# Scores of an attention in pieces of 512 and 256 keys instead of 384 and 384, contiguous in PSUM, with another order of the tasks

## The chip, the cores and the metric

One core of one Trainium2 chip. The metric is the device time of one execution in microseconds (us), lower is better. The times of the kernel before are the median of three runs; the trace is of one more execution, taken by the hardware profiler. TensorE is called PE in the rows, its weight loads PEld, VectorE DVE, ScalarE ACT, GpSimd POOL and SyncE, which issues the transfers, SP.

## The reference

```
kv_pool = kv.reshape(1, 96, 4, 8, 4, 128).mean(axis=(2, 4))   # 768 rows of 128
k = v = kv_pool.reshape(1, 768, 128) @ w_sr
s = (q @ k.T) / sqrt(128)                                     # q: 12288 x 128
a = exp(s - s.max(-1));  a /= a.sum(-1) + 1e-9
x = a @ v                                                     # 12288 x 128
h = x @ moe_w_in                                              # 128 -> 2048
g = where(h >= 1, h, where(h <= -1, 0, (h + 1)**2 / 4))
x2 = g @ moe_w_out                                            # 2048 -> 128
h2 = x2 @ moe2_w_in
out = (h2 * sigmoid(1.702 * h2)) @ moe2_w_out
```

All inputs and outputs are fp32.

## The kernel before

The 12288 queries are worked off in 24 **blocks** b of 512 (`TB`), each in four **tiles** t of 128 (`P`). All 768 keys (`NKEY`) stay on the chip as kT0 and kT1, a high and a low part. Nearly every product is split in this way for exactness: `mm3` (L349 to L352) does one product as three matmuls in fp32r, low times high, high times low, high times high (lines L350, L351, L352). Each matmul has its own load of a 128 x 128 stationary matrix.

For a tile of a block from the fourth on, `scores` (L729) does on TensorE `S_mm`: three matmuls on the first 384 keys (`HALF`) and three on the other 384, with the queries stationary. The tile S is one of three slots of two PSUM banks of 512 floats ("h" slots); each half stands at the beginning of a bank, so the tile is a [128, 2, 384] piece of a [128, 2, 512] slot. VectorE takes the row maximum (`S_max`, L743), ScalarE the exponential with its row sum (`S_exp`, L757). In `regular` ScalarE then writes the normalised high part Ph (L1125), VectorE the low part Pl (L1131), and VectorE transposes both in 32 x 32 squares into TT (L1140). SyncE sends each pair of tiles out to the array "turned" in device memory (L1161) and brings it back as PT_hi and PT_lo (L1173). TensorE then multiplies PT with V: that is pv of the block, which becomes x, split into xhi and xlo (L799, L346).

The MLPs follow with the same splits: h1 = x W1 into an h slot, 512 tokens x 256 hidden units at a time ("h1_8_7" is unit pair 7 of block 8), the activation u and its high and low parts ghi and glo on VectorE, ScalarE and GpSimd, and the product with O into an accumulator (acc1, L1244, L1245, L1247). The second MLP (h2, acc2) is alike. Blocks 0 to 3 take other paths: block 0 has code of its own with 384 keys at a time (S0_0x and S0_1x, maximum in L905, exponential in L912), blocks 1 to 3 write the exponentials over S in PSUM, transpose on TensorE and multiply in fp32 (L848). The weights (names W and O with the MLP's and the piece's number) are split on the chip while the first blocks run: conversions of a 128 x 512 piece in several steps on VectorE (L587, L593, L599, L606), ScalarE and GpSimd. Before all that, 4 x 4 patches of kv are summed (y, L414) and pooled on TensorE (L429, L431), and multiplied with w_sr (k_ps, L493, L521) to give kT (L502).

What order all this has on each engine is set by a planner before the program is built: each piece of work is a task with a key, and `Plan.order` takes for each engine the ready task with the least key for which its buffers are free by assumed durations:

```python
t.n, t.key = i, t.key + FINE.get(i, 0.0)
...
if best is None or (t.key, t.n) < (best.key, best.n):
    best = t
```

The keys come from a table `ORDER` (for instance `ATT_KEY` for the steps of the attention, `PAIR1` and `PAIR2` for those of the MLPs) and from `FINE`, one number for each of some thousand tasks.

Of the kernel before, what the change touches and what calls it, by code (L numbers as in the profile page):

```python
# [23 lines left out]
    REG_AT=2.93,  # L24
    STEP_AT=(0.54, 2.45, 0.5),
    ATT_KEY=(26.49, 2.85, 18.08, 13.03, -19.64, 10.84, 4.1, -15.3, 8.86, 57.26, -2.82),
    PAIR1=(3.65, -0.48, 3.27, 7.62, -6.74),
    PAIR2=(1.57, -6.31, 2.52, 13.5),
    ENDS=(7.48, -5.42),
# [1417 lines left out]
```

## Time and profile before

| | us |
|---|---|
| median of three runs (1303.97 to 1305.10) | 1304.73 |
| profiled execution, its own time | 1305.31 |
| its span from first to last instruction | 1303.6 |
| TensorE busy | 1291.9 (99%) |
| ScalarE busy | 1079.1 (83%) |
| GpSimd busy | 939.9 (72%) |
| VectorE busy | 910.2 (70%) |

The busy times are those of the whole span. A matmul's end is modelled in the trace and overlaps the next one's start, so what a matmul costs in a row of matmuls is read from one start to another. 5907 matmul records are in the trace; an fp32 matmul (L848, L429, L431, L864) leaves two.

### The profile page before, as it was taken

The page shows a single profiled execution, that of the slowest core. Times are in us where ns is not written, and L with a number is a line of the kernel's source. Part 1 is how long each engine was busy: PE and PEld are TensorE (multiplying, and loading weights), DVE is VectorE, ACT ScalarE, POOL GpSimd, SP SyncE. Part 2 cuts the span into 40 slices and gives each one's busy share as a digit, 9 for nine tenths or more (in the row PEclk, how much of TensorE's full clock was granted, in tenths as well). Part 3 has the DMA queues.
Part 4 walks back from the last instruction along what each step waited for, and adds up shares of the span by engine and source line. Part 5 has one row for each costly group of instructions (what it writes and reads, how often), then busy time and mean ns, then how long its engine had stood idle before and what let it go on. Part 6 is the DMA issues. An engine that isn't in the chain of part 4 may idle for free.

```text
span 1303.6 us, 16928 instructions
## 1 busy us (share of the span) xinstructions
PE 1291.9 (99%) x5907; PEld 1079.3 (83%) x5908; DVE 910.2 (70%) x1078; ACT 1079.1 (83%) x1265; POOL 939.9 (72%) x431
## 2 busy tenths in 40 slices
PE   9999999999999999999999999999999999999998
PEld 7868888888888888888888888888888888888886
DVE  4987676866777768767777677677776776775531
ACT  2878988888988888889888888898888888987765
POOL 4678886777766777777667767776677677766886
PEclk8999999999999999999999999999999999999999
DMA  9403155355445534554455344544553455333000
GB/s 339 147 9 93 22 172 135 105 150 148 124 114 168 133 111 114 150 146 117 113 170 136 108 120 146 144 115 113 170 138 105 128 146 144 100 106 105 1 9 17
DMA packets 166164, 157.42 MB, mean 121 GB/s; under 512 B 106304, under 2 KB 153024, under 8 KB 166080
## 3 DMA queue, kind: packets, MB, share of 16 engines
q1 hardware_dynamic: 165024, 156.21, 42.5%
q8 instruction: 48, 0.79, 0.3%
q14 instruction: 36, 0.29, 0.1%
q10 hardware_dynamic: 1056, 0.13, 0.1%
HBM read 85.52 MB, written 70.78 MB: 120 GB/s over the span
## 4 chain that ended last, share of the span: by engine, by line
PE 97%; DVE 1%; DMA 1%; issue 0%; SPq 0%; ACT 0%; DVEq 0%
PE h L350 13%; PE h L352 13%; PE h L351 13%; PE acc L1245 13%; PE acc L1247 13%; PE acc L1244 13%; PE S L350 3%; PE S L352 3%; PE S L351 3%; PE pv L352 2%; PE pv L351 2%; PE pv L350 2%; PE acc L1238 1%; PE pv L848 1%; DMA kv<-in_kv 1%
## 5 line engine op out<-in xcount | busy, mean ns | idle before, releaser
L346 POOL TENSOR_TENSOR glo<-u,ghi 128x1024 fp32r<-128x1024 f32 x350 | 837.0, 2409 | 300.4 <-ACT u L1334 135.1
L1274 DVE TENSOR_SCALAR u<-h 128x1024 f32<-128x1024 f32 x172 | 210.7, 1225 | 210.2 <-PE h L352 199.4
L1244 PE MATMUL acc<-ghi,O 128*128 128x512 f32 x752 | 293.7, 391 | 0.0
L1245 PE MATMUL acc<-ghi,O 128*128 128x512 f32 x752 | 293.3, 390 | 0.0
L1285 DVE SCALAR_TENSOR_TENSOR u<-h,u 128x1024 f32<-128x1024 f32 x192 | 233.7, 1218 | 82.1 <-ACT u L1281 76.1
L1328 ACT ACTIVATE ghi<-h 128x1024 fp32r<-128x1024 f32 x192 | 197.1, 1027 | 70.7 <-PE h L352 69.5
L1247 PE MATMUL acc<-glo,O 128*128 128x512 f32 x752 | 232.5, 390 | 0.0
L1281 ACT ACTIVATE u<-u 128x1024 f32<-128x1024 f32 x178 | 188.1, 1057 | 37.3 <-DVE u L1274 36.9
L1291 ACT ACTIVATE ghi<-u 128x1024 fp32r<-128x1024 f32 x184 | 194.8, 1060 | 7.2 <-PE acc L1245 3.5
L1334 ACT ACTIVATE u<-h 128x1024 f32<-128x1024 f32 x166 | 169.0, 1020 | 0.0
L1247 PEld LDWEIGHTS acc<-glo,O 128*128 128x128 f32 x752 | 141.1, 188 | 30.1
L1245 PEld LDWEIGHTS acc<-ghi,O 128*128 128x128 f32 x752 | 141.2, 188 | 27.3
L1244 PEld LDWEIGHTS acc<-ghi,O 128*128 128x128 f32 x752 | 141.2, 188 | 26.6
L350 PE MATMUL h<-xhi,W 128*128 128x512 f32 x384 | 151.2, 394 | 0.0
L351 PE MATMUL h<-xlo,W 128*128 128x512 f32 x384 | 149.7, 390 | 0.0
L352 PE MATMUL h<-xhi,W 128*128 128x512 f32 x384 | 149.7, 390 | 0.0
L351 PE MATMUL h<-x2lo,W 128*128 128x512 f32 x384 | 149.4, 389 | 0.0
L352 PE MATMUL h<-x2hi,W 128*128 128x512 f32 x384 | 149.4, 389 | 0.0
L350 PE MATMUL h<-x2hi,W 128*128 128x512 f32 x384 | 149.4, 389 | 0.0
L743 DVE TENSOR_REDUCE nm<-S 128x1 f32<-128x768 f32 x92 | 87.7, 953 | 9.3 <-PE S L352 7.0
L350 PEld LDWEIGHTS h<-xhi,W 128*128 128x128 f32 x384 | 72.1, 188 | 16.5 <-issue 1.3
L351 PEld LDWEIGHTS h<-xlo,W 128*128 128x128 f32 x384 | 72.1, 188 | 15.9 <-issue 0.7
(135 smaller groups left out, 1876.5 us busy)
## 6 DMA issues: line engine op xcount, KB each, us to landing
turned<-TT SPq DMA_DIRECT2D x82, 768.0 KB, 4.2
PT_lo<-turned SPq DMA_DIRECT2D x168, 192.0 KB, 4.6
PT_hi<-turned SPq DMA_DIRECT2D x160, 192.0 KB, 3.9
kv<-in_kv SPq DMA_DIRECT2D x12, 512.0 KB, 7.9
out<-o SPq DMA_DIRECT2D x94, 64.0 KB, 1.9
q<-in_q SPq DMA_DIRECT2D x92, 64.0 KB, 2.4
raw_W<-in_moe_w_in SPq DMA_DIRECT2D x8, 512.0 KB, 8.5
raw_O<-in_moe_w_out SPq DMA_DIRECT2D x8, 512.0 KB, 7.1
```

Of the source, the lines that this page charges most:

```text
L346: eng.tensor_tensor(out=lo, in0=full, in1=f32(hi), op=ALU.subtract)
L350: nc.tensor.matmul(ps, wl, xh, start=first, stop=False)
L351: nc.tensor.matmul(ps, wh, xl, start=False, stop=False)
L352: nc.tensor.matmul(ps, wh, xh, start=False, stop=last)
L1244: nc.tensor.matmul(acc, w[c][1], hi[:, c], start=k == 0 and c == 0, stop=False)
L1245: nc.tensor.matmul(acc, w[c][0], hi[:, c], start=False, stop=False)
L1247: nc.tensor.matmul(acc, w[c][0], lo[:, c], start=False, stop=k == NP - 1 and c == 1)
L1274: nc.vector.tensor_scalar(u, T["h", 1, b, k], -1.0, 1.0, ALU.max, ALU.add)
L1281: nc.scalar.activation(u, u, AF.Square, scale=1.0 if light else 0.5)
L1285: nc.vector.scalar_tensor_tensor(out=u, in0=T["h", 1, b, k], scalar=1.0, in1=u, op0=ALU.max, op1=ALU.min)
L1291: nc.scalar.activation(t, T["u", 1, b, k], AF.Copy)
L1328: nc.scalar.activation(t, T["h", 2, b, k], AF.Gelu_apprx_sigmoid)
```

## The change

The scores of a tile become three matmuls on keys 0 to 511 and three on keys 512 to 767. They now lie contiguous in the two banks, so that maximum, exponential, high and low part read one row of 768 in place of two of 384. Where the exponentials are written over S, the row sum goes into the last column of the second bank in place of the first. Block 0 keeps its halves of 384.

```diff
+    def flat(b, t):
+        return T["S", b, t].rearrange("p h k -> p (h k)")[:, :NKEY]
...
             for half in halves:
-                mm3(S[:, half, :HALF], cols, [k[:, half * HALF : (half + 1) * HALF] for k in kT], True, True)
+                r = slice(half * TB, min(NKEY, (half + 1) * TB))
+                mm3(flat(b, t)[:, r], cols, [k[:, r] for k in kT], True, True)
...
-            nc.vector.tensor_reduce(nm, T["S", b, t][:, :, :HALF], AX.XY, ALU.max, negate=True)
+            nc.vector.tensor_reduce(nm, flat(b, t), AX.X, ALU.max, negate=True)
...
-                sm = E[:, 0, 511:512]
-                p = E[:, :, :HALF]
+                sm = E[:, 1, TB - 1 : TB]
+                p = flat(b, t)
...
-            nc.scalar.activation(p, E[:, :, :HALF], AF.Exp, bias=T["nm", b, t], accum_out=sm)
+            nc.scalar.activation(p, flat(b, t), AF.Exp, bias=T["nm", b, t], accum_out=sm)
...
-                    nc.scalar.activation(
-                        p.rearrange("p (h k) -> p h k", h=2), T["S", b, t][:, :, :HALF], AF.Copy, scale=T["rd", b, t]
-                    )
+                    nc.scalar.activation(p, flat(b, t), AF.Copy, scale=T["rd", b, t])
...
-                        out=p.rearrange("p (h k) -> p h k", h=2), in0=T["S", b, t][:, :, :HALF],
-                        scalar=T["rd", b, t], in1=f32(T["Ph", b, t]).rearrange("p (h k) -> p h k", h=2),
+                        out=p, in0=flat(b, t), scalar=T["rd", b, t], in1=f32(T["Ph", b, t]),
```

Of the tables, `REG_AT`, `STEP_AT`, `ATT_KEY`, `PAIR1`, `PAIR2`, `ENDS` and the whole of `FINE` have new numbers; the assumed durations are the same:

```diff
-    ATT_KEY=(26.49, 2.85, 18.08, 13.03, -19.64, 10.84, 4.1, -15.3, 8.86, 57.26, -2.82),
-    PAIR1=(3.65, -0.48, 3.27, 7.62, -6.74),
+    ATT_KEY=(25.32, 1.79, -127.3, 116.38, -197.55, 82.12, -0.25, -285.85, -41.23, 2.7, -91.74),
+    PAIR1=(-299.59, 32.45, -80.73, -171.76, -17.68),
```

Some lines move by one to four: L350 to L352 of before are L351 to L353 of the change. What the numbers do is seen in the programs' instructions. In the order of before TensorE does 94 runs of score matmuls, 92 of one tile and 2 of two tiles in a row (four of them block 0's half tiles); in that of the change 83 runs, 70 of one and 13 of two.

First place: TensorE in block 10, tiles 2 and 3 (S10_2, S10_3). Before:

```order
L350 MATMUL S10_2_4472<-kT0_70,qlo10_4130 128x384
L351 MATMUL S10_2_4472<-kT1_71,qhi10_4126 128x384
L352 MATMUL S10_2_4472<-kT0_70,qhi10_4126 128x384
...
L1244 MATMUL acc1_8_4243<-ghi_4315,O11_609 128x512
...
L352 MATMUL h1_8_7_4494<-xhi8_3901,W13_577 128x512
L350 MATMUL S10_3_4505<-kT0_70,qlo10_4130 128x384
...
L352 MATMUL S10_3_4505<-kT0_70,qhi10_4126 128x384
L1244 MATMUL acc2_7_4445<-ghi_4443,O20_762 128x512
```

And in the change:

```order
L353 MATMUL S10_2_4481<-kT0_70,qhi10_4061 128x512
L351 MATMUL S10_2_4481<-kT0_70,qlo10_4080 128x256
L352 MATMUL S10_2_4481<-kT1_71,qhi10_4061 128x256
L353 MATMUL S10_2_4481<-kT0_70,qhi10_4061 128x256
L351 MATMUL S10_3_4490<-kT0_70,qlo10_4080 128x512
...
L353 MATMUL S10_3_4490<-kT0_70,qhi10_4061 128x256
L1244 MATMUL acc2_7_4445<-ghi_4443,O20_920 128x512
```

The twelve matmuls (six of acc1, six of h1) between the two tiles are gone from there. Blocks 6 to 10, 12, 14, 16, 18, 20, 21 and 23 are like this; elsewhere the tiles still stand apart.

Second place: TensorE, the first matmuls of pv10, the product of block 10's turned parts with V. Before they stand behind both first tiles of block 11:

```order
L352 MATMUL S11_1_4741<-kT0_70,qhi11_4601 128x384
...
L1245 MATMUL acc2_7_4445<-ghi_4713,O23_1180 128x512
L1247 MATMUL acc2_7_4445<-glo_4738,O23_1180 128x512 x2
L350 MATMUL pv10_4783<-PT10_hi_4407,V1_73 128x512
L351 MATMUL pv10_4783<-PT10_lo_4408,V0_72 128x512
```

In the change they stand between them, six matmuls of acc2 behind the first:

```order
L353 MATMUL S11_0_4706<-kT0_70,qhi11_4536 128x256
L1244 MATMUL acc2_7_4445<-ghi_4677,O22_1065 128x512
...
L1247 MATMUL acc2_7_4445<-glo_4696,O22_1065 128x512 x2
L351 MATMUL pv10_4728<-PT10_hi_4407,V1_73 128x512
L352 MATMUL pv10_4728<-PT10_lo_4408,V0_72 128x512
...
L351 MATMUL S11_1_4793<-kT0_70,qlo11_4551 128x512
```

From the beginning of S10_2 to pv10 there were 156 matmuls, 24 of them scores; now there are 120, 18 of them scores. Blocks 10, 12, 14, 16, 18 and 21 are like this.

Third place: TensorE at the start, block 0's scores of the first 384 keys, first half tiles (S0_00), and the pooling (pool_ps) of the last patches. Before:

```order
L429 MATMUL pool_ps_202<-pm_66,kv10_172 128x32 x4
L429 MATMUL pool_ps_202<-pm_66,kv11_181 128x32 x4
L431 MATMUL pool_ps_202<-pm_66,y9_212 128x32 x2
L431 MATMUL pool_ps_202<-pm_66,y10_221 128x32
L431 MATMUL pool_ps_202<-pm_66,y11_236 128x32
L350 MATMUL S0_00_255<-kT0_70,qlo0_240 128x384
```

In the change:

```order
L430 MATMUL pool_ps_202<-pm_66,kv10_172 128x32 x4
L351 MATMUL S0_00_234<-kT0_70,qlo0_231 128x384
...
L353 MATMUL S0_00_234<-kT0_70,qhi0_200 128x384
L432 MATMUL pool_ps_202<-pm_66,y9_212 128x32 x2
L432 MATMUL pool_ps_202<-pm_66,y10_221 128x32
L430 MATMUL pool_ps_202<-pm_66,kv11_181 128x32 x4
L494 MATMUL k_ps_266<-pT_260,wsr_68 128x256
L432 MATMUL pool_ps_202<-pm_66,y11_241 128x32
```

The six score matmuls go ahead of the last patches. On VectorE, the last conversions and maxima ahead of xlo0 (the low part of block 0's x), before:

```order
L606 SCALAR_TENSOR_TENSOR f_556<-raw_W13_407,i_494 128x512
...
L599 SCALAR_TENSOR_TENSOR i_563<-raw_O11_364,i_563 128x512
L606 SCALAR_TENSOR_TENSOR O1f_336<-raw_O11_364,i_563 128x512
L743 TENSOR_REDUCE nm_599<-S2_1_579 128x1
L346 TENSOR_TENSOR xlo0_591<-A0_1_444,xhi0_590 128x512
```

In the change:

```order
L600 SCALAR_TENSOR_TENSOR i_509<-raw_O21_348,i_509 128x512
...
L607 SCALAR_TENSOR_TENSOR f_575<-raw_O21_348,i_509 128x512
L347 TENSOR_TENSOR xlo0_562<-A0_1_446,xhi0_561 128x512
L747 TENSOR_REDUCE nm_588<-S2_0_564 128x1
```

The maximum of block 2's score tile stands behind xlo0 now; between the last part of kT and xlo0 VectorE had 20 conversion steps of 128 x 512, now 17. On TensorE, the ten matmuls that begin block 1's pv (L864, L848) stood just ahead of block 0's first h1 and stand behind it now.

## Rows read from the trace of the kernel before

**Rows 1.** The page: busy time by engine; the chain that ended last.

```profile
PE 1291.9 (99%) x5907; PEld 1079.3 (83%) x5908; DVE 910.2 (70%) x1078; ACT 1079.1 (83%) x1265; POOL 939.9 (72%) x431
...
PE 97%; DVE 1%; DMA 1%; issue 0%; SPq 0%; ACT 0%; DVEq 0%
```

**Rows 2.** Three stretches: us, busy (records) by engine, PEclk, DMA, GB/s.

```profile
29.60:55.60 26.00, 22.15 (x159) 19.95 (x159) 25.03 (x45) 23.12 (x52) 14.80 (x11) 1.00 0.72 230
55.60:120.00 64.40, 64.38 (x321) 50.39 (x320) 57.69 (x77) 51.35 (x74) 54.91 (x32) 1.00 0.05 9
120.00:1298.50 1178.50, 1178.41 (x5291) 987.35 (x5289) 814.17 (x944) 997.92 (x1127) 856.82 (x368) 1.00 0.43 119
```

**Rows 3.** Timeline of TensorE (start, duration) around one score tile of block 9.

```profile
606.26 0.39 PE L350 MATMUL h<-x2hi,W 128*128 128x512 f32 x1
...
611.70 0.33 PE L350 MATMUL S<-kT,qlo 128*128 128x384 f32 x1
...
612.77 0.39 PE L1244 MATMUL acc<-ghi,O 128*128 128x512 f32 x1
...
614.85 0.39 PE L350 MATMUL h<-xhi,W 128*128 128x512 f32 x1
```

**Rows 4.** The same around two score tiles in a row.

```profile
275.63 0.33 PE L350 MATMUL S<-kT,qlo 128*128 128x384 f32 x1
...
276.70 0.33 PE L350 MATMUL S<-kT,qlo 128*128 128x384 f32 x1
...
277.74 0.39 PE L350 MATMUL h<-xhi,W 128*128 128x512 f32 x1
```

**Rows 5.** TensorE at the start: blocks 0 and 1, and the first h1.

```profile
19.69 1.95 PE L429 MATMUL pool_ps<-pm,kv 128*128 128x32 f32 x16
21.47 1.78 PE L431 MATMUL pool_ps<-pm,y 128*128 128x32 f32 x8
23.07 0.67 PE L350 MATMUL S<-kT,qlo 128*128 128x384 f32 x1
...
25.13 1.05 PE L493 MATMUL k_ps<-pT,wsr 128*128 128x256 f32 x2
...
27.91 0.63 PE L493 MATMUL k_ps<-pT,wsr 128*128 128x128 f32 x2
...
53.78 0.65 PE L864 MATMUL pv<-ident,rd 128*128 128x128 f32 x4
...
54.27 1.50 PE L848 MATMUL pv<-PTf,Vf 128*128 128x128 f32 x12
...
55.57 0.49 PE L350 MATMUL h<-xhi,W 128*128 128x512 f32 x1
```

**Rows 6.** Two stretches of the start, columns as in the second group.

```profile
18.40:21.70 3.30, 3.30 (x32) 3.30 (x30) 2.54 (x5) 1.34 (x3) 2.44 (x5) 1.00 1.06 403
21.80:28.50 6.70, 6.70 (x24) 6.52 (x24) 2.24 (x4) 2.13 (x6) 1.63 (x1) 0.50 0.82 260
```

**Rows 7.** Timeline of VectorE at the start.

```profile
29.63 0.29 DVE L502 SCALAR_TENSOR_TENSOR kT<-k_ps,kT 128x128 fp32r<-128x128 f32 x1 [0.53 <-ACT kT L500]
...
37.52 0.69 DVE L606 SCALAR_TENSOR_TENSOR f<-raw_W,i 128x512 int32<-128x512 int32 x1
...
53.96 0.96 DVE L743 TENSOR_REDUCE nm<-S 128x1 f32<-128x768 f32 x1
...
54.84 0.68 DVE L346 TENSOR_TENSOR xlo<-A,xhi 128x512 fp32r<-128x512 f32 x1
```

**Rows 8.** Block 10's tile 2 to pv10: scores, transposes, transfers, pv.

```profile
638.39 0.33 PE L350 MATMUL S<-kT,qlo 128*128 128x384 f32 x1
...
653.79 0.94 DVE L1140 STREAM_TRANSPOSE TT<-Pl 128x768 f32<-128x768 f32 x1
...
653.90 1.20 SPq L1161 DMA_DIRECT2D turned<-TT  x2
...
659.23 1.73 SPq L1173 DMA_DIRECT2D PT_lo<-turned  x4
...
672.74 0.39 PE L350 MATMUL pv<-PT_hi,V 128*128 128x512 f32 x1
```

**Rows 9.** The page's issues of transfers: KB each, median us to landing.

```profile
turned<-TT SPq DMA_DIRECT2D x82, 768.0 KB, 4.2
PT_lo<-turned SPq DMA_DIRECT2D x168, 192.0 KB, 4.6
```

**Rows 10.** Tile PT_lo from 640 to 680 us: issue to landing.

```profile
DMA to landing us min/median/max: 4.5/5.8/6.4
```

More of the change, by code (lines that the diff above doesn't have):

```diff
@@ L23 @@
     ATT_GAP=((-33.53, -51.28), (-79.27, -28.22), (-105.65, -71.74), (74.87, -27.28)),
-    REG_AT=2.93,
-    STEP_AT=(0.54, 2.45, 0.5),
-    ATT_KEY=(26.49, 2.85, 18.08, 13.03, -19.64, 10.84, 4.1, -15.3, 8.86, 57.26, -2.82),
-    PAIR1=(3.65, -0.48, 3.27, 7.62, -6.74),
-    PAIR2=(1.57, -6.31, 2.52, 13.5),
-    ENDS=(7.48, -5.42),
+    REG_AT=2.99,
+    STEP_AT=(0.72, 1.72, 0.66),
+    ATT_KEY=(25.32, 1.79, -127.3, 116.38, -197.55, 82.12, -0.25, -285.85, -41.23, 2.7, -91.74),
+    PAIR1=(-299.59, 32.45, -80.73, -171.76, -17.68),
+    PAIR2=(28.1, -418.07, -297.44, 79.06),
+    ENDS=(368.8, -23.68),
     V_AT=(-206.47, -96.45),
@@ L735, in S_mm @@
                 T["S", b, t] = psum(sh, f"S{b}_{t}")
-            S = T["S", b, t]
             cols = [T[n, b][:, t * P : (t + 1) * P] for n in ("qhi", "qlo")]
             for half in halves:
-                mm3(S[:, half, :HALF], cols, [k[:, half * HALF : (half + 1) * HALF] for k in kT], True, True)
+                r = slice(half * TB, min(NKEY, (half + 1) * TB))
+                mm3(flat(b, t)[:, r], cols, [k[:, r] for k in kT], True, True)
         def S_max():
             nm = T["nm", b, t] = st.tile([P, 1], F32, tag="nm", bufs=4, name="nm")
-            nc.vector.tensor_reduce(nm, T["S", b, t][:, :, :HALF], AX.XY, ALU.max, negate=True)
+            nc.vector.tensor_reduce(nm, flat(b, t), AX.X, ALU.max, negate=True)
         def S_exp():
@@ L754, in S_exp @@
                 p = T["P", b, t] = slot(ph, [P, NKEY], F32, f"P{b}_{t}", "hi" if ph.room.name == "P" else "")
-                p = p.rearrange("p (h k) -> p h k", h=2)
             T["sm", b, t] = sm
-            nc.scalar.activation(p, E[:, :, :HALF], AF.Exp, bias=T["nm", b, t], accum_out=sm)
+            nc.scalar.activation(p, flat(b, t), AF.Exp, bias=T["nm", b, t], accum_out=sm)
         def recip():
```

195 rows, old and new, of the table FINE are left out of this document.

## The prediction, written before the changed kernel ran

> **What bounds the kernel now.** I first read the page's busy times and the chain that ended last [rows 1]. TensorE is busy 99% of the span and makes up 97% of the chain; the next engine, ScalarE, stands at 83%. An average over the span hides stages, so I then asked for stretches [rows 2]. The reader should see three things there. From 120 us to the last stage TensorE is busy 1178.41 of 1178.50 us and from 55.6 to 120 us 64.38 of 64.40: whatever the other engines save there is worth nothing, and only fewer or shorter matmuls, or a new wait, move the end. From 29.6 to 55.6 us it is busy 22.15 of 26.0, so 3.85 us are idle, while VectorE is busy 25.03: this is the one stage, behind the first loads, that VectorE sets. And the granted clock is 1.00 in all three. The change can therefore act in three places: the price of a score tile, the 3.85 us, and new holes in the dense part.
>
> Since ends of matmuls are modelled, I price them from start to start. From 606.26 to 611.70 lie 24 matmuls of 512 columns [rows 3]: 0.2267 us each. Of two score tiles in a row the second goes from 276.70 to 277.74 [rows 4]: 1.04 us, 0.1733 for 384 columns.
>
> **The scores.** 23 blocks of four tiles, 92 tiles, change their form. A line through the two prices (0.0533 us per 128 columns) puts 256 columns at 0.120 us. The new tile is then 3 x 0.2267 + 3 x 0.120 = 1.04 us, and the old one 6 x 0.1733 = 1.04: no gain in steady running, since the columns are the same 2304. The rows bound the 256: not above the 0.1733 of 384 columns, which would add 92 x 3 x 0.0533 = 14.7 us; not below the records of 128 columns, twelve of which pass from 54.27 to 55.57 [rows 5], 0.108 us each, which would save 92 x 3 x 0.012 = 3.3 us. In the latter rows the weight load of each record is hidden behind another's stream at 0.108 us, and 0.120 is longer than that, so I take the line's value.
>
> The Trainium skill (TensorE: Matmul & The Clock Gate, section LDWEIGHTS) puts a load at its columns divided by 1.2, in ns: 107 ns for 128 columns, about what a stream of 256 columns takes. Were the load not hidden behind another stream, a tile would be an estimated 3 x 0.107 = 0.32 us dearer, 29 us for the 92 tiles; with the load hidden, nothing. The trace's 0.108 us for load and stream of a record together [rows 5] speaks for the latter.
>
> A lone tile costs more than its steady price. Its six matmuls take 1.07 us (611.70 to 612.77) and the nine matmuls of 512 behind them 2.08 (612.77 to 614.85) in place of 9 x 0.2267 = 2.04 [rows 3]. Of two tiles in a row the first takes 1.07, the second 1.04 [rows 4]. So each run of score matmuls pays 0.03 + 0.04, about 0.06 us in the mean, at the changes of width, and there were 94 runs, 5.6 us in all. The order has 11 runs fewer: 11 x 0.06 = 0.66 saved. What the 79 runs with the new widths pay isn't in the trace: the first three matmuls now have the neighbours' width, but there is a step from 512 to 256 inside a tile. Bounds: nothing is left of it (-5.6 in all), or each of the 79 pays double (79 x 0.06 = +4.7, less 0.66: +4.1). I take 0.01 less for each, 0.8: **-1.5 us**.
>
> **Maximum, exponential, high and low part** read 768 contiguous columns. Their rows belong to VectorE (70%) and ScalarE (83%), whose work is hidden behind TensorE from 55.6 us on [rows 1, 2]: I take 0. The cover is gone only in the start, where six or so maxima of blocks 1 and 2 stand; one has a duration of 0.96 us [rows 7], and even a tenth off each would be 0.6 us.
>
> **The start.** VectorE works without a gap from the last part of kT (29.63) to xlo0 (54.84), and h1 starts at 55.57 [rows 5, 7]. Three things move.
> First, 17 conversion steps of 128 x 512 in place of 20 stand in this stretch, and the maximum of a tile of block 2 stands behind xlo0: 3 x 0.69 and 0.88 (53.96 to 54.84) [rows 7], 2.95 us earlier.
> Second, kT's last part comes later. TensorE's granted clock was 1.00 from 18.4 to 21.7 and 0.50 from 21.8 to 28.5 [rows 6], that is 2.4 and 1.2 GHz. At the former, sixteen pooling records took 19.69 to 21.47 or about 0.11 us each, at the latter eight took 21.47 to 23.07 or 0.20 each [rows 5]. In the change the six scores of S0_00 (2.06 us, 23.07 to 25.13) go ahead of kv11's eight records, which so fall into the slow stretch: about 8 x 0.09 = 0.7 later. S0_00 may also find TensorE idle ahead of it, until qlo0 is there; I allow 1.1 us for that, as long as five or six of the slow records, which is a choice and in no row. So +0.7 to +1.8, middle +1.25.
> Third, block 1's first ten pv matmuls filled 53.78 to 55.57 ahead of h1 [rows 5]. Behind h1 they take their 1.8 us from the dense part, and leave a hole: +1.8.
> Together -2.95 + 1.25 + 1.8 = +0.1, between -0.45 and +0.65. The rest of that stage is reordered on all engines, and I can't follow each conversion: a piece of W ready 2 us later holds up the second or third h1. Bounds: of the 3.85 us idle about 3 can go (-3), and as much can be added (+3). Since the weights whose conversions VectorE did before xlo0 are now due later, the risk lies above: I take **+0.35**.
>
> **The wait for the turned parts.** For block 10, S10_2 starts at 638.39, VectorE ends the last transpose at 654.73 (653.79 + 0.94), SyncE sends TT out from 653.90, and the last of PT_lo is issued until 660.96 (659.23 + 1.73); pv starts at 672.74 [rows 8], 34.35 us after S10_2. Landing takes 6.4 us at most [rows 10]: 667.4 at the latest, 5.3 us early. In the change 120 matmuls lie between: 102 of 512 columns, 9 and 9 of the scores: 111 x 0.2267 + 9 x 0.120 = 26.2 us, and pv's second matmul, the first to read PT_lo, comes at 26.5. PT_lo had landed 29.0 after S10_2 at the latest; by the medians of 4.2 and 4.6 us [rows 9] (654.73, 4.2, 1.73 and 4.6) it is 26.9. Tile 3 stands twelve matmuls, 2.7 us, earlier, but the transposes of VectorE come as room and their place in its queue allow; I take 0.3 us of that for the last one. The wait would be 26.6 - 26.5 = 0.1 us, with bounds of 0 (all of the 2.7 reaches the last transpose) and 2.2 (28.7, the slowest landing). Behind the waiting matmul stands all of TensorE; nothing else fills in. Six blocks are so: 6 x 0.1 = **+0.6 us**, bounds 0 and 13.2. In the other blocks 156 matmuls or nearly as many remain, and 5 us to spare.
> The transfers that come with an earlier transpose collide with none new: there are as many, in the same order on SyncE's queue.
>
> **The h slots.** Two tiles in a row hold two of three slots until their low parts are read. The order puts products for acc behind them, which need no slot, so I cost this at 0. What hides it is those six to twelve matmuls (1.4 to 2.7 us); without them the next h waits for the exponential.
>
> **The sum**: -1.5 + 0.35 + 0.6 = -0.55 us. The profiled execution's span becomes 1303.05 and its own time 1304.76; this execution was 0.58 above the median of 1304.73, so the median becomes **1304.2**.
>
> **Rivals.**
> *A, no change* (within 0.2%, 2.6 us, about what a measurement of this kernel can tell from none): the sum above. For it speaks a TensorE at 1178.41 of 1178.50 us whose columns stay the same [rows 2]. 0.44.
> *B, faster*: the changes of width cost little with 512 beside 512, say -4 in place of -1.5, and the start closes part of its 3.85 us. With -4, -1 and +0.6 it is 1300.3 us. For it speaks that the first half of the new tile has its neighbours' width; against it that the step is then inside each tile. 0.34.
> *C, slower by the wait for PT_lo*: it decides from a landing later than 26.5 us after the block's tile 2. At the slowest landing of 28.7 the six blocks give 13.2 in place of 0.6: 1316.8; at 27.5 each waits 1.0, and it is 1309.6. For it speak that VectorE's queue, not the scores, sets the last transpose, and the 5.8 us that block 10's own landings had in the median [rows 10]; against it the tiles' 2.7 us. 0.13.
> *D, slower by the weight loads*: 256 columns take as long as 384 did, +14.7, 1318.9. Against it the 0.108 us of a record with its load [rows 5]. 0.05.
> *E, a start that is later*: +3 in place of 0.35 gives 1306.9, and slightly more is slower by the bound. 0.04.
> So faster 0.34, same 0.44, slower 0.22. The range: down to 1300.3, where B lies (a tenth below it), and up to 1309, which holds A, E and C's milder half; the rest of C and D lie above. For case A alone it is 1302.1 to 1306.7.
>
> **What the trace would show.** The scores: starts 0.120 us apart for the 256 columns and 1.04 to 1.07 for a tile; 0.17 would be D. Width changes: nine matmuls of 512 behind a tile in 2.04 (B) or 2.08. The start: first h1 before 55.57 by about 1.7 us with TensorE's idle time from 29.6 on near 3.9 us; xlo0 as the last thing it waits for. The wait: an idle stretch of TensorE put down to PT_lo in blocks 10, 12, 14, 16, 18 and 21; idle from 120 us on of 0.1 us says there is none, over 3 us is C. The forecast is wrong if the 256 columns aren't on the line, if the second or third h1 waits for a late piece of W, or if the transposes don't follow the scores.

## The result and the profile after

The changed kernel takes 1319.51 us (median, 1319.08 to 1319.76); the kernel before took 1304.86 in the same comparison: ratio 1.0113, interval 1.0096 to 1.0131. It is 1.1% slower, 14.65 us, outside the range that was forecast.

The three stretches of the trace of after, with columns as in [rows 2], answer to those rows:

```profile
29.60:55.60 26.00, 22.17 (x133) 19.81 (x132) 23.04 (x39) 19.85 (x42) 14.54 (x10) 0.87 0.72 229
55.60:120.00 64.40, 63.65 (x326) 49.51 (x324) 57.11 (x75) 51.05 (x74) 54.78 (x32) 1.00 0.05 8
120.00:1310.00 1190.00, 1181.02 (x5285) 971.95 (x5284) 817.05 (x947) 997.91 (x1128) 853.98 (x368) 1.00 0.44 118
```

Where TensorE had been busy 1178.41 of 1178.50 us it is now idle for 8.98 of 1190. What ended those waits is in the list of TensorE's waits of after (total us, how often, longest):

```profile
PE h L351 <- ACT u L1334: 5.0, 8, 0.7
PE h L351 <- DVE glo L347: 2.3, 7, 0.6
...
PE h L351 <- DVE u L1285: 1.5, 6, 0.3
...
PE pv L352 <- DMA PT_lo<-turned: 0.2, 1, 0.2
```

21 of the 22 waits from 120 us on are those of h matmuls for whoever reads an h slot last: ScalarE's second gelu (L1334), the low part that VectorE forms from h (L347), the last step of MLP 1 (L1285). PT_lo, on which the forecast's price of a wait lay, is waited for once. Idle time understates them, since a matmul's end is modelled; TensorE's rows around one of the longest kind (block 11's second h1, h1_11_1; timeline of after; the first row is the beginning of block 12's tiles 2 and 3, which stand in a row):

```profile
590.28 0.39 PE L351 MATMUL S<-kT,qlo 128*128 128x512 f32 x1
...
600.54 0.39 PE L351 MATMUL h<-x2hi,W 128*128 128x512 f32 x1
...
601.90 0.39 PE L351 MATMUL h<-xhi,W 128*128 128x512 f32 x1
...
603.26 0.39 PE L351 MATMUL h<-x2hi,W 128*128 128x512 f32 x1
...
604.62 0.39 PE L1244 MATMUL acc<-ghi,O 128*128 128x512 f32 x1
...
605.75 0.39 PE L1247 MATMUL acc<-glo,O 128*128 128x512 f32 x1
606.81 0.50 PE L351 MATMUL h<-xhi,W 128*128 128x512 f32 x1 [0.67 <-ACT u L1334]
...
607.62 0.40 PE L351 MATMUL h<-xhi,W 128*128 128x512 f32 x1
...
1312.02 0.62 PE L1247 MATMUL acc<-glo,O 128*128 128x512 f32 x2
```

(The last row, the last products, is there for the length of the dense part below.) From 605.75 to 606.81 it is 1.06 us where a matmul takes 0.227: 0.83 lost for 0.67 of idle. The three matmuls behind it take 0.81 (606.81 to 607.62) in place of 0.68: another 0.13. All 22 waits, measured so, are 12.5 us, and with the 0.09 to 0.13 that the three matmuls behind each lose 14.8.

Three h pairs start in a row at 600.54, 601.90 and 603.26, one product group follows, and at 605.98 TensorE wants the slot that it began to fill at 600.54. ScalarE's timeline of after tells why it isn't free:

```profile
597.99 1.06 ACT L1281 ACTIVATE u<-u 128x1024 f32<-128x1024 f32 x1 [0.18 <-DVE u L1274]
598.96 0.88 ACT L1128 ACTIVATE Ph<-S,rd 128x768 fp32r<-128x768 f32 x1
601.22 1.06 ACT L1291 ACTIVATE ghi<-u 128x1024 fp32r<-128x1024 f32 x1 [1.38 <-DVE u L1285]
602.30 1.28 ACT L1328 ACT_TABLE_LOAD   x1
603.60 1.03 ACT L1328 ACTIVATE ghi<-h 128x1024 fp32r<-128x1024 f32 x1
604.79 1.06 ACT L1281 ACTIVATE u<-u 128x1024 f32<-128x1024 f32 x1 [0.17 <-DVE u L1274]
605.76 1.00 ACT L1334 ACTIVATE u<-h 128x1024 f32<-128x1024 f32 x1
```

It worked through the attention's exponentials and high parts, then stood 1.38 us for VectorE's L1285, then loaded the gelu's table (1.28 us), and read the h of 600.54 only from 603.60 on. The last reader ends at 606.76: the slot was held 6.2 us. VectorE's L1285 was late since it stood behind a low part and a transpose of the attention (timeline of VectorE, after):

```profile
598.13 1.00 DVE L1132 SCALAR_TENSOR_TENSOR Pl<-S,rd,Ph 128x768 fp32r<-128x768 f32 x1
599.05 0.97 DVE L1140 STREAM_TRANSPOSE TT<-Ph 128x768 f32<-128x768 f32 x1
599.94 1.19 DVE L1285 SCALAR_TENSOR_TENSOR u<-h,u 128x1024 f32<-128x1024 f32 x1
```

### The profile page after: what moved, and what is told of

It is laid out like the page before. It is cut to its first block, busy times and chain, and to the rows that moved or that the text cites. A ratio compares the mean times of both kernels' runs of the same rounds, so it can differ in the third digit from the quotient of the medians.

```text
span 1317.4 us, 16886 instructions
## 1 busy us (share of the span) xinstructions
PE 1295.2 (98%) x5907; PEld 1062.6 (81%) x5908; DVE 913.2 (69%) x1078; ACT 1077.9 (82%) x1265; POOL 938.5 (71%) x431
## 4 chain that ended last, share of the span: by engine, by line
PE 90%; DVE 3%; ACT 2%; DMA 2%; SPq 1%; issue 1%; POOL 0%; DVEq 0%; ACTq 0%
PE h L351 13%; PE h L353 12%; PE h L352 12%; PE acc L1245 12%; PE acc L1244 12%; PE acc L1247 12%; PE S L353 2%; PE S L352 2%; PE S L351 2%; PE pv L352 2%; PE pv L353 2%; PE pv L351 2%; PE acc L1238 1%; DVE u L1274 1%; DVE TT L1140 1%; PE pv L851 1%
## 5 line engine op out<-in xcount | busy, mean ns | idle before, releaser
L347 POOL TENSOR_TENSOR glo<-u,ghi 128x1024 fp32r<-128x1024 f32 x350 | 835.8, 2408 | 335.3 <-ACT u L1334 166.3
L1285 DVE SCALAR_TENSOR_TENSOR u<-h,u 128x1024 f32<-128x1024 f32 x192 | 233.6, 1217 | 90.0 <-ACT u L1281 85.6
L1334 ACT ACTIVATE u<-h 128x1024 f32<-128x1024 f32 x166 | 169.2, 1021 | 0.0
L351 PE MATMUL h<-xhi,W 128*128 128x512 f32 x384 | 154.4, 402 | 6.5 <-ACT u L1334 4.8
L351 PE MATMUL h<-x2hi,W 128*128 128x512 f32 x384 | 150.3, 391 | 2.3 <-DVE u L1285 1.5
L352 PE MATMUL h<-xlo,W 128*128 128x512 f32 x384 | 149.8, 390 | 0.0
L353 PE MATMUL h<-xhi,W 128*128 128x512 f32 x384 | 149.7, 390 | 0.0
L352 PE MATMUL h<-x2lo,W 128*128 128x512 f32 x384 | 149.5, 389 | 0.0
L353 PE MATMUL h<-x2hi,W 128*128 128x512 f32 x384 | 149.5, 389 | 0.0
L351 PEld LDWEIGHTS h<-xhi,W 128*128 128x128 f32 x384 | 72.1, 188 | 28.7 <-ACT u L1334 7.9
L351 PEld LDWEIGHTS h<-x2hi,W 128*128 128x128 f32 x384 | 72.1, 188 | 20.3 <-PE h L353 3.9
```

Of the source, the lines that this page charges most:

```text
L347: eng.tensor_tensor(out=lo, in0=full, in1=f32(hi), op=ALU.subtract)
L351: nc.tensor.matmul(ps, wl, xh, start=first, stop=False)
L352: nc.tensor.matmul(ps, wh, xl, start=False, stop=False)
L353: nc.tensor.matmul(ps, wh, xh, start=False, stop=last)
L1285: nc.vector.scalar_tensor_tensor(out=u, in0=T["h", 1, b, k], scalar=1.0, in1=u, op0=ALU.max, op1=ALU.min)
```

## The experiments

Theory O: the new order costs the time by waits for h slots, and the new pieces save some. Rival P: the pieces cost it. In the table, "dense" is from the first h matmul to the start of the row of the last products in the profiled execution, in us, 1242.2 before and 1257.8 after.

| run | median us | ratio to before, interval | dense |
|---|---|---|---|
| e1_shape | 1300.95 | 0.9967 (0.9955 to 0.9980) | 1238.4 |
| e2_order | 1321.53 | 1.0130 (1.0115 to 1.0146) | 1260.3 |
| e3_step | 1303.89 | 0.9991 (0.9982 to 1.0000) | 1241.6 |
| e4_apart | 1313.32 | 1.0064 (1.0052 to 1.0077) | 1251.4 |
| e5_rank | 1301.14 | 0.9975 (0.9963 to 0.9986) | 1238.4 |
| e6_near | 1306.70 | 1.0017 (1.0009 to 1.0026) | 1244.8 |
| e7_start | 1301.28 | 0.9977 (0.9968 to 0.9986) | 1238.7 |
| e8_swap | 1319.76 | 1.0114 (1.0100 to 1.0127) | 1257.9 |
| e9_short_first | 1300.51 | 0.9964 (0.9951 to 0.9978) | 1238.4 |
| e10_rows | 1301.04 | 0.9979 (0.9970 to 0.9988) | 1238.4 |

**Pieces alone (e1_shape).** The kernel before with the first diff of the section on the change, tables untouched; of it the core:

```diff
-                mm3(S[:, half, :HALF], cols, [k[:, half * HALF : (half + 1) * HALF] for k in kT], True, True)
+                r = slice(half * TB, min(NKEY, (half + 1) * TB))
+                mm3(flat(b, t)[:, r], cols, [k[:, r] for k in kT], True, True)
```

> The new score pieces (512 and 256 columns, contiguous) in the order of the kernel before; tables untouched. Theory O (the order of the steady blocks costs the time, the pieces save some): the trace of the change shows a lone score tile in 1.03 us and the nine matmuls of 512 behind it in 2.07, so a run of scores pays about 0.04 us less than before, 94 runs 3.6 us: 1301.3 us, between 1300.4 and 1302.4, with no idle time of TensorE from 120 us on. Theory P (the pieces cost the time: tiles of 256 columns, or readers of the contiguous tile, keep h slots longer): 1312 to 1320 us with idle TensorE in front of h.

1300.95: theory O. TensorE has no idle time from 120 us on:

```profile
120.00:1292.00 1172.00, 1172.00 (x5279) 973.54 (x5277) 812.79 (x942) 995.11 (x1124) 854.69 (x366) 1.00 0.43 120
```

A lone tile, from its timeline, stands at 503.68 to 504.72, 1.04 us, and nine matmuls of 512 behind it take 2.06 (to 506.78), where [rows 3] had 1.07 and 2.08:

```profile
503.68 0.39 PE L350 MATMUL S<-kT,qlo 128*128 128x512 f32 x1
...
504.36 0.28 PE L350 MATMUL S<-kT,qlo 128*128 128x256 f32 x1
...
504.72 0.40 PE L1243 MATMUL acc<-ghi,O 128*128 128x512 f32 x1
...
506.78 0.39 PE L350 MATMUL h<-xhi,W 128*128 128x512 f32 x1
```

256 columns cost (504.72 - 504.36) / 3 = 0.12 us.

**Order alone (e2_order).** The changed tables with the old pieces.

```diff
-                mm3(flat(b, t)[:, r], cols, [k[:, r] for k in kT], True, True)
+                mm3(S[:, half, :HALF], cols, [k[:, half * HALF : (half + 1) * HALF] for k in kT], True, True)
```

> The new tables with the old score pieces (384 and 384). Theory O: all the waits of the change are there (about 22 in front of h, 12.5 us from start to start), and the runs of scores pay what they paid before: 1319.5 + 3.3 = 1322.8 us, between 1321 and 1325. Theory P: without the pieces no waits, 1304 to 1308 us.

1321.53, with the same 21 waits for h slots; the one for PT_lo isn't there. Theory P falls: the pieces save time in both orders (4.0 us alone, 2.0 in the change).

**One number set back (e3_step).**

```diff
-    STEP_AT=(0.72, 1.72, 0.66),
+    STEP_AT=(0.72, 2.45, 0.66),
```

> The change with one number set back: the second of STEP_AT, 2.45 in place of 1.72, the rank of the first MLP's products against the h matmuls (0.73 steps of 6.77 us later). Theory O in its narrow form (products ranked early are used up, and TensorE has nothing left to do when h waits for a slot): the 22 waits of the steady part go, 12.5 us and about 22 x 0.13 = 2.9 us of slow starts behind them: 1304.1 us, between 1303 and 1305.5. If it is the two tiles in a row, or another number of the tables, the waits stay: 1314 to 1320 us. This also sets the tiles apart in the built order, so the next run is needed to tell the two.

1303.89. One short wait is left from 120 us on (columns as above), and the dense stretch is 16.2 us shorter:

```profile
120.00:1294.00 1174.00, 1173.78 (x5285) 974.44 (x5283) 815.16 (x942) 997.62 (x1126) 855.17 (x367) 1.00 0.43 120
```

**Tiles apart (e4_apart).** The change with ATT_KEY's second number set back.

```diff
-    ATT_KEY=(25.32, 1.79, -127.3, 116.38, -197.55, 82.12, -0.25, -285.85, -41.23, 2.7, -91.74),
+    ATT_KEY=(25.32, 2.85, -127.3, 116.38, -197.55, 82.12, -0.25, -285.85, -41.23, 2.7, -91.74),
```

> The change with the distance of a pair's two tiles set back (ATT_KEY's second number, 2.85 in place of 1.79): 94 runs of one tile and one of two in place of 13 of two; STEP_AT as in the change. Theory O, narrow: the waits stay, 8 to 15 us of them, 1314 to 1322 us. Theory T (two score tiles in a row hold two of three h slots, and that is what h waits for): the waits go, 1303 to 1306 us.

1313.32, just below what theory O gave: theory T falls as the whole cause, since hardly any tiles stand in a row and much of the loss is there: 9.8 us of dense time over the run before. It lies in other waits than those of the change. The trace lists three of h, 0.7 us together; most are shorter and not listed. Once a block an h matmul starts 0.47 us behind the matmul ahead in place of 0.23, as at 605.55 (TensorE's timeline of this run):

```profile
604.85 0.61 PE L1247 MATMUL acc<-glo,O 128*128 128x512 f32 x2
605.55 0.50 PE L351 MATMUL h<-x2hi,W 128*128 128x512 f32 x1
```

In the change itself, blocks 6 to 9, which have tiles in a row too, had no wait either (its waits begin at 500 us, but for one of 0.2). And 12 of its 21 waits for slots stand behind the tiles of blocks 11, 13, 15, 17, 19 and 22, which stand apart; for block 11 (timeline of TensorE, after; two tiles, two waits):

```profile
537.38 0.39 PE L351 MATMUL S<-kT,qlo 128*128 128x512 f32 x1
...
539.80 0.39 PE L351 MATMUL S<-kT,qlo 128*128 128x512 f32 x1
...
554.88 0.47 PE L351 MATMUL h<-x2hi,W 128*128 128x512 f32 x1 [0.26 <-DVE u L1285]
...
558.15 0.47 PE L351 MATMUL h<-xhi,W 128*128 128x512 f32 x1 [0.30 <-DVE glo L347]
```

The long waits (0.67 and 0.73) do stand behind tiles in a row, those of blocks 10, 12, 14, 16, 18, 21 and 23, and they are gone here. This run moves more than the tiles, so a part for them isn't excluded.

**The number in the other tables (e5_rank).** The first experiment with 1.72.

```diff
-    STEP_AT=(0.54, 2.45, 0.5),
+    STEP_AT=(0.54, 1.72, 0.5),
```

> The order of the kernel before with the new pieces (as in the first experiment) and only STEP_AT's second number changed to 1.72. In the built order one can count what TensorE has in reserve: pairs of h1 issued less product groups of the first MLP issued, averaged over TensorE's work in blocks 9 to 19. It is 2.84 in the first experiment, 2.79 in the change with 2.45, 2.55 in the change, 2.33 in the change with tiles apart; here 2.82. Theory R (what counts is the reserve that the tables leave together, not the number): no waits from 120 us on, 1301 us, 1300 to 1302. Theory N (the number 1.72 itself spends the products early): waits in front of h, 1306 to 1316 us.

1301.14, dense as in the first experiment: the number alone, theory N, falls. It costs only with the other new tables.

**The other number in the old tables (e6_near).** The first experiment with ATT_KEY's second number changed.

```diff
-    ATT_KEY=(26.49, 2.85, 18.08, 13.03, -19.64, 10.84, 4.1, -15.3, 8.86, 57.26, -2.82),
+    ATT_KEY=(26.49, 1.79, 18.08, 13.03, -19.64, 10.84, 4.1, -15.3, 8.86, 57.26, -2.82),
```

> The order of the kernel before with the new pieces and only ATT_KEY's second number changed to 1.79 (the two tiles of a pair ranked nearer). The built order has 90 runs of one tile and three of two, and a reserve of 2.28 pairs. Theory R: waits in front of h as with the tiles apart or more, 8 to 16 us, 1309 to 1317 us. Theory T (two tiles in a row are what costs): hardly any are in a row, so 1301 to 1302 us. Theory N: STEP_AT is that of before, so 1301 us.

1306.70: waits, as theory R has it and T and N don't, but 6.4 us of them where 8 to 16 were expected. Here the count of the reserve told that there are waits, not how long they are. Most are too short to show as idle: in TensorE's timeline of this run h starts 0.28 after the matmul ahead, with no wait noted, and the next 0.31 later, once a block:

```profile
609.73 0.39 PE L352 MATMUL h<-x2hi,W 128*128 128x512 f32 x1
610.01 0.47 PE L350 MATMUL h<-xhi,W 128*128 128x512 f32 x1
610.32 0.40 PE L351 MATMUL h<-xlo,W 128*128 128x512 f32 x1
```

**The start of before (e7_start).** In a sketch, with E the tasks planned ahead of 160 us and STEP_AT as in e3_step:

```diff
-FINE = after
+FINE = {n: (before if n in E else after)[n]}
```

> The change with STEP_AT's second number at 2.45 and, for all tasks that are planned ahead of 160 us, the numbers of FINE of the kernel before. If the new order of the start costs the 2.9 us by which the change with 2.45 alone is above the first experiment (block 1's pv behind the first h, a wait of 0.8 us at about 58 us), this runs as the first experiment does: 1301.3 us, 1300.3 to 1302.3. If those 2.9 us lie in the steady part: 1303.9 us.

1301.28: the new order of the start costs 2.6 us by the medians (1303.89 - 1301.28) and 1.8 by the ratios, which compare each with its own runs of before. The rest of the order costs next to nothing once the waits are gone (dense 1238.7 against 1238.4 in e1_shape).

**One pair exchanged on ScalarE (e8_swap).** Behind the planner, in its list, at the six places:

```diff
+        for s, f in zip(act, act[1:]):
+            if s.name[:1] == ("square",) and f.name[:1] == ("full",) and s.name[2] == 0 and f.name[2] == 3 and f.name[1] >= 6:
+                out.remove(s)
+                out.insert(out.index(f) + 1, s)
```

> The change with one pair of ScalarE's instructions exchanged at six places, nothing else: where h of an odd block's first unit waits longest (0.67 us of idle, at 500, 607, 713, 819, 925 and 1083 us), the square of the newer h1 (L1281) stood ahead of the last reader of the older h2 (L1334), which lets its slot go. Theory Q (the slot is free late because ScalarE works in the order written, and the reader stands behind a square that itself waits for VectorE): the six waits go, 0.83 us from start to start and 0.13 of slow start each, 5.8 us: 1313.7 us, between 1312.5 and 1315. If the reader waits for something else (its own buffer u, GpSimd) or the wait only moves on to the next h: 1317 to 1320 us.

1319.76. The long waits are gone from the six places, and two shorter ones of 0.39 and about 0.35 stand behind each instead. The first is for VectorE's step on the square that was put back (timeline of TensorE of this run, where L1285 is L1290):

```profile
607.14 0.47 PE L356 MATMUL h<-x2hi,W 128*128 128x512 f32 x1 [0.39 <-DVE u L1290]
```

So the reader's place in ScalarE's queue does set when the slot comes free, but this isn't the cause: the work that is late is only late elsewhere.

**Short piece first (e9_short_first).** The first experiment with the loop over the pieces turned round.

```diff
-            for half in halves:
+            for half in (1, 0):
```

> The first experiment (new pieces, order of before) with the three matmuls of 256 ahead of the three of 512 in each tile. If a change of width costs wherever it stands, the number of changes is the same and so is the time: 1301 us, 1300 to 1302. If the gain of the new pieces comes from entering a tile at the neighbours' width, about 94 x 0.03 = 2.8 us are lost: 1303.8 us.

1300.51, the same as the first experiment within their spreads. Where the change of width stands makes no difference.

**Three h pairs in a row, with the reserve kept (e10_rows).**

```diff
-            t.n, t.key = i, t.key + FINE.get(i, 0.0)
+            t.n, t.key = i, t.key + FINE.get(i, 0.0) - (2.84 if i in range(482, 1316, 49) else 0.0)
```

> The first experiment with the last score tile of each block from the seventh on ranked 2.84 nearer to the tile ahead of it. In the built order this gives 20 places with three h pairs in a row (three in the first experiment, 18 in the change, 4 in the change with 2.45), followed by one product group and the next h, just as at the longest waits of the change; the reserve is 2.82. Theory L (local: three h in a row take all three slots, and one product group isn't enough until the first comes free): waits at 17 or more places, 0.5 to 0.9 us each, 1310 to 1317 us. Theory R (the reserve of products covers it): no waits, 1300 to 1302 us.

1301.04, no wait: theory L falls. The same row of h pairs stands in its TensorE timeline at 593.28, 594.64 and 596.00, one product group, and the fourth comes at 598.72, 5.44 us after the first, without a wait. Its ScalarE is done with the attention earlier:

```profile
589.38 1.06 ACT L1280 ACTIVATE u<-u 128x1024 f32<-128x1024 f32 x1
590.34 1.68 ACT L1127 ACTIVATE Ph<-S,rd 128x768 fp32r<-128x768 f32 x2
591.90 1.06 ACT L1290 ACTIVATE ghi<-u 128x1024 fp32r<-128x1024 f32 x1
...
593.50 1.28 ACT L1327 ACT_TABLE_LOAD   x1
594.84 1.03 ACT L1327 ACTIVATE ghi<-h 128x1024 fp32r<-128x1024 f32 x1
595.76 1.02 ACT L1333 ACTIVATE u<-h 128x1024 f32<-128x1024 f32 x1
```

The slot of 593.28 is free at 596.78, after 3.5 us. Here block 10's last h1 (h1_10_7) came directly behind block 12's last score tile, at 586.46, with four product groups after it. VectorE took its last step (L1284) at 590.47, ahead of the low parts:

```profile
590.47 1.22 DVE L1284 SCALAR_TENSOR_TENSOR u<-h,u 128x1024 f32<-128x1024 f32 x1 [0.61 <-ACT u L1280]
591.61 1.93 DVE L1131 SCALAR_TENSOR_TENSOR Pl<-S,rd,Ph 128x768 fp32r<-128x768 f32 x2
```

In the change two product groups went ahead of that h (592.36 to 595.10, 2.7 us), and L1285 fell behind the attention's steps.

## Why the prediction was wrong

**The h slots: this step failed.** "I cost this at 0", it said of the wait for slots, and looked only at what stands directly behind two tiles in a row. The longest waits stand some 15 us behind the tiles (590.28 and 606.81 above), after the whole group of attention steps, and all of them cost 14.8 us (15.6 by the medians of the change and e3_step). The front's orders showed two tiles in a row without the six product and six h matmuls between; what follows them on ScalarE and VectorE wasn't followed to the next h. The forecast had no rival of this kind, either.

What caused it is shown as far as this: with the new tables TensorE takes products of the first MLP sooner and asks for h later. The reserve that e5_rank counts, pairs of h1 issued less product groups taken, fell from 2.84 to 2.55 in the mean. The five orders with 2.79 or more that ran have no such waits, or one (e1, e3, e5, e7, e10); the three with 2.55 or less that ran have them (the change 14.8 us, e4 9.8, e6 6.4). The set of numbers does it together: in the change, setting back STEP_AT's number is enough (e3) and setting back ATT_KEY's isn't (e4); in the tables of before the one does nothing (e5), the other something (e6). That the reserve goes with the waits is shown; that it causes them isn't. That it goes by h pairs that come late, meet the attention's steps and hold slots 6.2 us in place of 3.5 is read from the two traces at one kind of place; it wasn't tried alone. Why 2.33 and 2.28 cost less than 2.55 stays open.

**The scores**: right in kind, the size off. -1.5 was taken with -5.6 as the bound; -4.0 was measured in the old order (1304.90 to 1300.95; dense -3.8) and -2.0 in the new (1321.53 to 1319.51; dense -2.5), which has 83 runs of scores in place of 94; what makes up the rest of the difference isn't shown. The 0.120 us of 256 columns, read off a line through 384 and 512, held. The term that was mis-sized is what the new widths save at each run: 0.01 was taken, and 1.07 + 2.08 against 1.04 + 2.06 is 0.05. Rival D (weight loads as the bound of 256 columns) fell with the 0.12 us. By the Trainium skill (TensorE: Matmul & The Clock Gate, section LDWEIGHTS) a load of 128 columns is an estimated 107 ns. The 0.12 us for load and stream together agree with a load that is hidden. The trace's own records of loads last 0.19 us and overlap: in the tile of e1_shape they start 0.12 us apart, so they don't tell what a load alone takes. The 0 for the readers of the tile was right: a maximum takes 953 ns in the mean before and in e1_shape, over two rows of 384 as over one of 768.

**The start**: +0.35 taken, +1.8 to +2.6 measured (e7_start), within its bounds, but two of its three parts were off. The first was 2.95 us less of VectorE's work between kT's last part and xlo0. VectorE's timeline of after has these at 26.95 and 52.11, 25.16 us apart, as in [rows 7] (29.63 to 54.84, 25.21): it had less to do (23.04 us busy from 29.6 to 55.6, against 25.03 in [rows 2]) and waited instead.

```profile
26.95 0.29 DVE L503 SCALAR_TENSOR_TENSOR kT<-k_ps,kT 128x128 fp32r<-128x128 f32 x1 [0.44 <-ACT kT L501]
...
52.11 0.69 DVE L347 TENSOR_TENSOR xlo<-A,xhi 128x512 fp32r<-128x512 f32 x1
```

Two executions don't settle it: over all traces that distance is 25.21 to 27.64 us with the old start and 23.85 to 26.48 with the new one, 1.3 less in the mean, with a spread as wide within each.

The second, kT 1.25 us later, rested on the granted clock of one execution. kT is 2.7 us earlier in after, but there the clock was 1.00 from 18.4 to 34 us, where [rows 6] had 0.50 from 21.8 to 28.5, and the order of before doesn't bring that slow stretch by itself: e1_shape, with the old start, has 1.00 as well, and kT as early (a stretch with columns as above; VectorE's timeline).

```profile
18.40:28.50 10.10, 9.17 (x67) 8.66 (x67) 6.99 (x11) 5.71 (x17) 4.22 (x5) 1.00 0.92 311
...
26.68 0.29 DVE L502 SCALAR_TENSOR_TENSOR kT<-k_ps,kT 128x128 fp32r<-128x128 f32 x1 [0.41 <-ACT kT L500]
```

In the traces without that slow stretch kT's last part starts at 26.24 to 26.98 with the old start (e1, e6, e9, e10) and at 26.80 to 27.27 with the new one (after, e2, e3, e4, e8): 0.36 later in the mean. So at one clock the sign was right and the size too large. In the three traces with it (before, e5, e7, all with the old start) kT comes at 28.49 to 29.63. Whether the new start makes it rarer (none of five traces has it, against three of seven) stays open.

After had slow stretches later: 0.50 from 40.1 to 43.5, and 0.51 (1.2 GHz) from 50.3 to 53.6, behind one in which TensorE was busy 1.90 of 3.20 us:

```profile
18.40:34.00 15.60, 13.76 (x103) 12.98 (x102) 11.96 (x18) 9.97 (x27) 7.75 (x8) 1.00 0.96 328
...
47.00:50.20 3.20, 1.90 (x12) 1.11 (x10) 3.20 (x8) 3.04 (x8) 3.11 (x3) 1.00 0.36 62
50.30:53.60 3.30, 3.30 (x14) 3.01 (x14) 2.43 (x6) 3.06 (x6) 0.33 (x1) 0.51 0.14 23
```

There a score tile and a transpose of the attention stood ahead of the first h, which so came at 54.22, though xlo0 was done at 52.80 (timeline of TensorE, after):

```profile
53.53 0.94 PE L839 MATMUL T<-ident,P 128*128 128x128 f32 x6
54.22 0.48 PE L351 MATMUL h<-xhi,W 128*128 128x512 f32 x1
...
58.37 1.60 PE L851 MATMUL pv<-PTf,Vf 128*128 128x128 f32 x12 [0.75 <-ACT rds L872]
```

The third part was right: block 1's pv went behind h1 for 1.8 us, and a wait of 0.75 with it (58.37). In this execution that makes -1.35 + 1.8 + 0.8 = +1.25. The runs say 1.8 to 2.6; the first h lies between 51.89 and 54.67 in the profiled executions with the new start and between 52.95 and 55.97 in those with the old one, so one execution of each doesn't settle the parts.

**The wait for the turned parts**: 0.6 taken, one wait of 0.2 us measured in six blocks. Rival C fell: a time near its 1316.8 came out by luck, by another wait. The measured sum is -4.0 + 2.6 + 14.8 (in which that wait stands) = 13.4, near the 14.65. By the runs alone, the change lies 15.6 above e3_step, that 2.6 above e7_start, and that 3.3 below its before: 14.9.

## What to carry to other kernels

When an order changes, look for the wait of the busiest engine not at the moved instruction but at the next places where it needs a buffer back, and follow the readers of that buffer on each in-order queue to their last step. Count what the engine has in reserve (work issued ahead less work taken): here 0.3 of a pair less in the mean went with 21 waits. And before a cost is taken from one trace of a start, see in a second one whether its clock comes again: here it didn't always, with one order of the start. And time the parts apart before judging the whole: the pieces alone are 0.33% faster than before (0.36% with the short piece first), the best that ran.

## What the runs showed of the hardware

A matmul that waits less than about 0.16 us leaves no idle time in the rows, because its forerunner's end is modelled 0.39 us behind its start, where the next can start 0.227 behind: in e6_near the dense part is 6.4 us longer than in e1_shape, and the trace notes three waits of h with 2.3 us together. Idle time of 0.09 us isn't noted as a wait either (e4_apart, 605.55). Starts have to be compared. After a wait the next three matmuls cost 0.09 to 0.13 us more in all. A tile of six matmuls of 384 columns between matmuls of 512 costs 0.04 to 0.05 us more, with the nine behind it, than one of three of 512 and three of 256, whichever three come first.
